# Hedgehog attention and an ELU feed-forward layer on one core: groups of four heads, DMA transposes and exact query maxima in place of head pairs and TensorE transposes

## Chip, cores and metric

The kernel runs on one core of a Trainium2 chip. The metric is the time of one execution on the device in microseconds (us); lower is better. TensorE is called PE below, VectorE DVE, ScalarE ACT, GpSimd POOL and SyncE SP.

## The reference

q, k and v are 8 batches x 8 heads x 576 tokens x 64, all float32.

```
def phi(x):                                   # x: b h s d
    proj = x @ w_phi                          # 64 -> 128
    proj = proj - max(|proj|, last axis)
    return concat([exp(proj), exp(-proj)])    # 256 features
q_p, k_p = phi(q), phi(k)
kv  = k_p^T v                                 # 256 x 64 for each head
z   = sum of k_p over the tokens
x   = (q_p kv) / (q_p z + 1e-6)               # tokens x 64
x   = heads side by side                      # 4608 x 512
h   = x @ moe_w_in                            # 512 -> 2048
g   = where(h > 0, h, exp(min(h, 0)) - 1)
out = g @ moe_w_out                           # 4608 x 512, float32
```

## The kernel before

**Attention** works on a pair of heads at a time (`emit_attention_pair`, 4 pairs x 8 batches = 32). Twelve DMAs on POOL's queue load q, k and v of the pair and cast them to bf16; token t*128+p goes to partition p, so that each run in DRAM is one token of one head, 64 floats or 256 bytes. PE transposes q and k against an identity (L198), ACT or DVE copies the result out (L199). For k, a matmul of K=128 against the zero-padded `w_phi_both` projects both heads of 128 tokens (L212); DVE takes the row maxima (L220), ACT the two exponentials (L227, L230) and exp(-m), exp(m) (L233, L237), and DVE multiplies v by them (L243). For q the projection comes out with features on partitions (L259) and ACT takes two exponentials (L266, L268); with `EXACT_QMAX = False` the maxima of q are not subtracted, so the two halves of q's features enter with equal weight. Then come kv (L276), the numerator and denominator (L341), the division on DVE (L351 to L353), a PE transpose of x (L369) and copies into `xT_sb` (L371, L375), which holds all 4608 tokens.

**Feed-forward** ("moe") works in 9 chunks of 512 tokens. `moe_mm1_unit` (16 in a chunk) does four matmuls of 512 columns (L102), exp on ACT (L110), min and subtract on DVE (L112) and a maximum with the PSUM tile on DVE (L116). `moe_mm2_unit` (4 in a chunk) does sixteen matmuls (L127), copies the result and stores it from SP's queue.

**Order.** Batches run in turn; after each pair some feed-forward units are emitted, `len(pending) // remaining_pairs` of them, so that few come early and many late. What is left follows at the end. The tile framework plans the final order on each engine at build time: it starts from this order and moves an instruction ahead where its inputs and buffers are ready in its plan. `nc.any` copies go to ACT or DVE as planned. PSUM has five banks for attention and three for feed-forward. Both weight matrices are loaded before the first pair (L84, L88), on the same queue as the pair's loads.

## Time and profile before

| | us |
|---|---|
| runs | 525.71, 530.53, 530.68 (median 530.53) |
| span of the profiled execution | 524.4 |
| PE busy | 408.5 (78%) |
| DVE busy | 364.1 (69%) |
| ACT busy | 319.5 (61%) |
| POOL busy | 258.3 (49%) |

The span runs from the first to the last instruction of one profiled execution. That execution's own time is not given beside it; the runs stand 1.3 to 6.3 us above the span, the median 6.1. The busy share of an engine is an average over stages that have different limits, so the rows below are taken stage by stage.

### The profile page before, as it was taken

Reading aid. Unit: us, or ns where it says so; the run is one execution under the profiler, and the core shown is the slowest. Engines: PE = TensorE matmul, PEld = TensorE weight load, DVE = VectorE, ACT = ScalarE, POOL = GpSimd, SP = SyncE. Lnnn points to the kernel's source line nnn. Section 1 sums busy time; section 2 is a strip of 40 time slices with the busy share of each in tenths; the row PEclk is TensorE's granted clock in tenths of the full one; section 3 lists DMA queues with packets and bytes.
Section 4 is the critical chain, followed back from the end, with each engine's and each line's share of the span. In section 5 each row is a group of like instructions: output and inputs, shape, how many; then the busy total and the mean of one; then the engine's idle time right before and its main releaser. Section 6 shows DMA issues by size and latency. Waiting matters only on the chain.

```text
span 524.4 us, 9742 instructions
## 1 busy us (share of the span) xinstructions
PE 408.5 (78%) x3200; PEld 222.5 (42%) x3200; DVE 364.1 (69%) x1358; ACT 319.5 (61%) x904; POOL 258.3 (49%) x400
## 2 busy tenths in 40 slices
PE   0056667678976679977789778977997999989997
PEld 0034444345543345534455444443544454434433
DVE  2055568989788988798986789479459579174470
ACT  0046568777568876787866788479257367153441
POOL 6299999967677767776676666460000000000000
PEclk9997668979989989998999899999999999989999
DMA  8989988955866756877567655660110100200102
GB/s 157 185 53 59 58 57 55 58 40 38 106 61 40 46 37 62 100 46 46 36 56 85 58 35 34 90 59 2 42 40 2 56 25 1 81 1 31 51 0 80
DMA packets 124817, 28.45 MB, mean 54 GB/s; under 512 B 117600, under 2 KB 119648, under 8 KB 124768
## 3 DMA queue, kind: packets, MB, share of 16 engines
q0 software_dynamic: 119584, 18.41, 47.7%
q1 hardware_dynamic: 5184, 9.44, 4.9%
q8 instruction: 25, 0.41, 0.3%
q14 instruction: 24, 0.20, 0.1%
HBM read 36.77 MB, written 9.44 MB: 88 GB/s over the span
## 4 chain that ended last, share of the span: by engine, by line
PE 49%; DVE 21%; ACT 21%; DMA 4%; issue 3%; POOL 1%; POOLq 0%; DVEq 0%; ACTq 0%
PE po L127 21%; PE ph L102 13%; DVE vs L243 5%; ACT EK L230 4%; ACT EK L227 4%; PE pk L212 4%; DVE gT L116 4%; DVE u_sb L112 4%; ACT Eq L266 4%; DVE x_pair L353 3%; DMA w_out_sb<-in_moe_w_out_dram 3%; PE pn L341 3%; PE tr L198 3%; ACT Eq L268 2%; PE xt L369 2%
## 5 line engine op out<-in xcount | busy, mean ns | idle before, releaser
L102 PE MATMUL ph<-xT_sb,w_in_sb 128*128 128x512 bf16 x576 | 158.9, 396 | 19.3 <-DVE gT L116 15.7
L127 PE MATMUL po<-w_out_sb,gT 128*128 128x512 bf16 x576 | 133.4, 379 | 0.3 <-DVE gT L116 0.2
L110 ACT ACTIVATE e_sb<-ph 128x512 f32<-128x512 f32 x144 | 85.2, 640 | 39.5 <-PE ph L102 39.1
L116 DVE TENSOR_TENSOR gT<-u_sb,ph 128x512 bf16<-128x512 bf16 x144 | 97.2, 681 | 1.8
L112 DVE TENSOR_SCALAR u_sb<-e_sb 128x512 bf16<-128x512 f32 x144 | 62.3, 442 | 42.4 <-ACT e_sb L110 41.8
L102 PEld LDWEIGHTS <-w_in_sb 128*128 128x128 bf16 x576 | 55.4, 101 | 75.8 <-issue 39.3
L243 DVE TENSOR_TENSOR vs<-v_aug,em 128x130 bf16<-128x130 bf16 (+1 forms) x384 | 75.6, 265 | 9.6 <-ACT em L233 9.1
L127 PEld LDWEIGHTS <-gT 128*128 128x128 bf16 x576 | 54.3, 98 | 59.6 <-issue 3.6
L168 POOL DMA_DIRECT2D q_pair<-in_q_dram x64 | 55.2, 866 | 43.4 <-PE tr L198 37.8
L266 ACT ACTIVATE Eq<-pq 128x288 bf16<-128x288 f32 x128 | 59.1, 462 | 24.6 <-PE pq L259 24.3
L220 DVE TENSOR_REDUCE m_k<-pk 128x4 f32<-128x512 f32 (+1 forms) x96 | 52.1, 594 | 14.3 <-PE pk L212 14.2
L268 ACT ACTIVATE Eq<-pq 128x288 bf16<-128x288 f32 x128 | 60.9, 476 | 0.0
L168 POOL DMA_DIRECT2D k_pair<-in_k_dram x64 | 57.1, 898 | 5.1 <-DMA w_out_sb<-in_moe_w_out_dram 4.4
L184 POOL DMA_DIRECT2D v_aug<-in_v_dram x64 | 53.7, 863 | 10.0 <-DVE den L351 5.2
L227 ACT ACTIVATE EK<-pk 128x512 bf16<-128x512 f32 (+1 forms) x96 | 52.5, 547 | 4.5 <-DVE m_k L220 4.5
L188 POOL DMA_DIRECT2D v_aug<-in_v_dram x64 | 40.8, 639 | 27.8 <-DVE vs L243 27.8
L276 PEld LDWEIGHTS <-EK 128*128 128x128 bf16 x640 | 32.4, 102 | 51.2 <-issue 20.1
L135 ACT COPY o_sb<-po 128x512 f32<-128x512 f32 x27 | 15.8, 586 | 62.0 <-PE po L127 62.0
L230 ACT ACTIVATE EK<-pk 128x512 bf16<-128x512 f32 (+1 forms) x96 | 53.5, 558 | 0.0
L259 PE MATMUL pq<-qTp,w_phi_both 128*128 128x288 bf16 x128 | 32.6, 300 | 19.9 <-ACT EK L230 18.6
L276 PE MATMUL pkv<-vs,EK 128*128 128x65 bf16 x640 | 36.1, 201 | 14.4 <-ACT EK L230 8.0
L174 POOL DMA_DIRECT2D k_pair<-in_k_dram x64 | 43.9, 685 | 4.5 <-DMA w_out_sb<-in_moe_w_out_dram 4.5
(46 smaller groups left out, 458.4 us busy)
## 6 DMA issues: line engine op xcount, KB each, us to landing
out_dram<-o_sb SPq DMA_DIRECT2D x36, 256.0 KB, 2.0
q_pair<-in_q_dram POOLq DMA_DIRECT2D x64, 64.0 KB, 2.6
k_pair<-in_k_dram POOLq DMA_DIRECT2D x64, 64.0 KB, 2.7
v_aug<-in_v_dram POOLq DMA_DIRECT2D x64, 64.0 KB, 2.8
w_in_sb<-in_moe_w_in_dram POOLq DMA_DIRECT2D x4, 512.0 KB, 7.1
w_out_sb<-in_moe_w_out_dram POOLq DMA_DIRECT2D x4, 512.0 KB, 15.9
q_pair<-in_q_dram POOLq DMA_DIRECT2D x64, 8.0 KB, 2.1
k_pair<-in_k_dram POOLq DMA_DIRECT2D x64, 8.0 KB, 2.3
```

The costliest lines, as they stand in the source:

```text
L102: nc.tensor.matmul(ph[:, 0:csz], w_in_sb[:, ct, jt * P:(jt + 1) * P], xT_sb[:, ct, t0:t0 + csz], start=(ct == 0), stop=(ct == N_CT - 1),)
L110: nc.scalar.activation(e_sb[:, 0:csz], ph[:, 0:csz], ACT.Exp)
L112: nc.vector.tensor_scalar(u_sb[:, 0:csz], e_sb[:, 0:csz], 1.0, 1.0, op0=ALU.min, op1=ALU.subtract,)
L116: nc.vector.tensor_tensor(gT[:, jt, 0:csz], u_sb[:, 0:csz], ph[:, 0:csz], op=ALU.max)
L127: nc.tensor.matmul(po[0:tsz], gT[:, jt, tt * P:tt * P + tsz], w_out_sb[:, jt, :], start=(jt == 0), stop=(jt == N_JT - 1),)
L168: nc.gpsimd.dma_start(out=dst[:, 0:full_st, hi * D:(hi + 1) * D], in_=src[b, h, 0:full_st * P, :].rearrange("(t p) d -> p t d", p=P),)
L227: nc.scalar.activation(EK[:, g0:g0 + gcnt, :, 0, :], pk_v, ACT.Exp, scale=1.0)
L230: nc.scalar.activation(EK[:, g0:g0 + gcnt, :, 1, :], pk_v, ACT.Exp, scale=-1.0)
L243: nc.vector.tensor_tensor(vs[hi][:, sg, g0:g0 + gcnt], v_aug[hi][:, g0:g0 + gcnt], em[:, sg, g0:g0 + gcnt, hi:hi + 1].to_broadcast((P, gcn ...
L266: nc.scalar.activation(eq[:, 0, c0:c0 + half_S], pq, ACT.Exp, scale=1.0)
L268: nc.scalar.activation(eq[:, 1, c0:c0 + half_S], pq, ACT.Exp, scale=-1.0)
L276: nc.tensor.matmul(pkv[:, hi, sg, :], EK[:, ti, hi, sg, :], vs[hi][:, sg, ti, :], start=(ti == 0), stop=(ti == n_st - 1),)
```

## The change

**Attention** works on groups of four heads (16 groups, two for each batch). One DMA per tensor and batch loads the first 512 tokens of all 8 heads, with token 4p+s on partition p, so that a run in DRAM is four tokens, 1 KB; two more load the last 64 tokens of each head. All transposes are DMA transposes on SP's queue: q and k (`transposes`), the query maxima (`mT`), and x straight into `xT_sb`; the identity, the PE transposes and their copies are gone. After a transpose, even and odd token blocks lie on partitions 0 to 63 and 64 to 127, and each projection is a matmul of K=64 on its half of the array's rows (`project`, `stage_q`). The maxima of q are computed (`stage_qmax`: a projection and a reduction as for k), split into a high and a low bf16 part, transposed, and subtracted in PSUM by matmuls with a matrix `sel` of -1 and 0. The multiplication of v moves from DVE to POOL. Exponentials and reductions act on 768 columns in two PSUM banks.

**Feed-forward.** The ELU becomes exp on ACT, min on POOL, and add and max in one DVE instruction. The sixteen matmuls of an output tile are cut into four parts. The copies of the output go to ACT. The store order follows the new token order.

**Order.** The pieces of group n are interleaved with those of group n+1, and 16 feed-forward units are spread over each group; a chunk joins the list four pieces after its batch. Loads run two batches ahead on POOL's queue. The first q and k are loaded before the weights. PSUM has two tiles of two banks for attention (`pj`) and four banks for feed-forward and kv.

```diff
+    def load_full(name, src, b, h0, h1):
+        if (name, b) not in natural:
+            natural[name, b] = (
+                io.tile([P, H, 4 * D], BF16, name=name + "f"),
+                io.tile([P, H // 2, D], BF16, name=name + "m"),
+            )
+        nc.gpsimd.dma_start(
+            out=natural[name, b][0][:, h0:h1, :],
+            in_=src[b, h0:h1, 0:FULL, :].rearrange("h (p s) d -> p h (s d)", s=4),
+        )
+    def load_mixed(name, src, b):
+        pairs = src[b, :, FULL:S, :].rearrange("(pr hi) p d -> hi p pr d", hi=2)
+        for hi in range(2):
+            nc.gpsimd.dma_start(
+                out=natural[name, b][1][hi * D:(hi + 1) * D, :, :], in_=pairs[hi]
+            )
...
+    for g in range(2):
+        for name, src in (("k", k), ("q", q)):
+            load_full(name, src, 0, g * GH, (g + 1) * GH)
+            if g == 0:
+                load_mixed(name, src, 0)
+    load("v", v, 0)
...
+    load("k", k, 1)
+    load("q", q, 1)
+    load("v", v, 1)
...
+    sel = consts.tile([P, NI, F], BF16)
+    nc.vector.memset(sel, 0.0)
+    for off in (0, NI, D, D + NI):
+        nc.gpsimd.affine_select(
+            out=sel, in_=sel, pattern=[[-1, NI], [0, F]],
+            compare_op=ALU.not_equal, fill=-1.0, base=-off, channel_multiplier=1,
+        )
...
+        e_sb = epool.tile([P, CHUNK], FP32, name="e_sb")
+        nc.scalar.activation(e_sb, ph, ACT.Exp)
+        nc.gpsimd.tensor_scalar(
+            e_sb, e_sb, 1.0, 0.0, op0=ALU.min, op1=ALU.max
+        )
+        nc.vector.scalar_tensor_tensor(
+            gT[:, jt, :], e_sb, -1.0, ph, op0=ALU.add, op1=ALU.max
+        )
...
+    def transposes(n):
+        if n >= NG:
+            return
+        b, g = divmod(n, 2)
+        for name in ("k", "q"):
+            full, mixed = natural[name, b]
+            dst = tpool.tile([P, NI, P], BF16, name=name + "T")
+            nc.sync.dma_start_transpose(
+                out=dst[:, 1:NI, :],
+                in_=full[:, g * GH:(g + 1) * GH, :].rearrange("p h x -> p (h x)"),
+            )
+            nc.sync.dma_start_transpose(
+                out=dst[:, 0:1, :],
+                in_=mixed[:, 2 * g:2 * g + 2, :].rearrange("p h x -> p (h x)"),
+            )
+            st[name + "T", n] = dst
+    def project(xT, c):
+        pj = pjp.tile([P, 2, 4, P], FP32, name="pj", tag="pj")
+        for i3 in range(3):
+            for par in range(2):
                 nc.tensor.matmul(
+                    pj[:, par, i3, :],
+                    xT[par * D:(par + 1) * D, 3 * c + i3, :],
+                    w2[par * D:(par + 1) * D, :],
                     start=True,
                     stop=True,
                 )
+        return pj[:, :, 0:3, :]
+    def stage_k(n, c):
...
+        pj = project(st["kT", n], c)
+        row_max(mk, pj, c)
+        for sg in range(2):
             nc.scalar.activation(
+                EK[:, sg, :, 3 * c:3 * c + 3, :], pj, ACT.Exp, scale=1.0 - 2.0 * sg
+            )
+        if c < 2:
+            return
...
+        nc.gpsimd.tensor_tensor(
+            vs[:, :, :, 0:D],
+            vf[:, g * GH:(g + 1) * GH, :]
+            .rearrange("p h (s d) -> p (h s) d", s=4)
+            .unsqueeze(1).to_broadcast((P, 2, 4 * GH, D)),
+            em[:, :, 2:2 * NI].unsqueeze(3).to_broadcast((P, 2, 4 * GH, D)),
+            op=ALU.mult,
+        )
+        nc.gpsimd.tensor_copy(vs[:, :, :, D], em[:, :, 2:2 * NI])
+        for hi in range(2):
+            r = slice(hi * D, (hi + 1) * D)
+            nc.gpsimd.tensor_tensor(
+                vsm[r, :, :, hi, 0:D],
+                vm[r, 2 * g:2 * g + 2, :].unsqueeze(1).to_broadcast((D, 2, 2, D)),
+                em[r, :, 0:2].unsqueeze(3).to_broadcast((D, 2, 2, D)),
+                op=ALU.mult,
+            )
+            nc.gpsimd.tensor_copy(vsm[r, :, :, hi, D], em[r, :, 0:2])
+    def stage_qmax(n, c):
...
+        pj = project(st["qT", n], c)
+        row_max(mq, pj, c)
+        if c < 2:
+            return
...
+        nc.sync.dma_start_transpose(out=mT, in_=mhl.rearrange("p r x -> p (r x)"))
+    def stage_q(n, c):
...
+        for par in range(2):
+            r = slice(par * D, (par + 1) * D)
+            nc.tensor.matmul(
+                pj[:, par, 0:3 * P],
+                w2[r, :],
+                qT[r, 3 * c:3 * c + 3, :].rearrange("p i t -> p (i t)"),
+                start=True,
+                stop=False,
+            )
+        for i3 in range(3):
+            for par in range(2):
+                r = slice(par * D, (par + 1) * D)
+                nc.tensor.matmul(
+                    pj[:, par, i3 * P:(i3 + 1) * P],
+                    sel[r, 3 * c + i3, :],
+                    mT[r, 0, :],
+                    start=False,
+                    stop=(i3 == 2),
+                )
+        for sg in range(2):
             nc.scalar.activation(
+                Eq[:, sg, :, 3 * c * P:3 * (c + 1) * P], pj[:, :, 0:3 * P], ACT.Exp,
+                scale=1.0 - 2.0 * sg,
+            )
+    def stage_pn(n, pr):
...
+        nc.sync.dma_start_transpose(
+            out=xT_sb[:, ct, full_col(b):full_col(b) + FULL].rearrange(
+                "p (t r) -> p t r", t=4
+            ),
+            in_=xp[:, 0:4].rearrange("p t h d -> p (t h d)"),
+        )
+        nc.sync.dma_start_transpose(
+            out=xT_sb[:, ct, mixed_col(b):mixed_col(b) + D].rearrange(
+                "p (t r) -> p t r", t=1
+            ),
+            in_=xp[0:D, 4].rearrange("p h d -> p (h d)"),
+        )
+    for n in range(NG):
...
+        pieces = []
+        for c in range(3):
+            pieces.append((stage_q, n, c))
+            if nxt:
+                pieces.append((stage_qmax, n + 1, c))
+        pieces.append((transposes, n + 2))
+        for pr in range(2):
+            pieces.append((stage_kv, n, pr))
+        if nxt:
+            pieces.append((stage_k, n + 1, 0))
+        pieces.append((stage_pn, n, 0))
+        if nxt:
+            pieces.append((stage_k, n + 1, 1))
+        pieces.append((stage_pn, n, 1))
+        if nxt:
+            pieces.append((stage_k, n + 1, 2))
...
+        for j, (fn, *args) in enumerate(pieces):
+            fn(*args)
+            after_piece()
+            want = 16 * (j + 1) // len(pieces)
+            while done < want:
+                emit_moe()
+                done += 1
```

## Rows read from the trace of the kernel before

**Rows 1.** The page's parts 1 and 2: busy us by engine; tenths in 40 slices.

```profile
PE 408.5 (78%) x3200; PEld 222.5 (42%) x3200; DVE 364.1 (69%) x1358; ACT 319.5 (61%) x904; POOL 258.3 (49%) x400
...
PE   0056667678976679977789778977997999989997
...
POOL 6299999967677767776676666460000000000000
...
DMA  8989988955866756877567655660110100200102
```

**Rows 2.** Timeline, first work of PE: start, us, engine, line, idle before.

```profile
26.93 0.69 PE L198 MATMUL tr<-ident,q_pair 128*128 128x128 bf16 x5 [26.93 <-DMA q_pair<-in_q_dram]
```

**Rows 3.** Busy us by stretch: PE, PEld, DVE, ACT, POOL; clock, DMA share, GB/s.

```profile
62.80:74.40 11.60, 7.17 (x70) 5.16 (x69) 7.01 (x33) 7.06 (x23) 11.60 (x19) 0.65 0.91 59
...
210.00:262.00 52.00, 40.94 (x384) 23.51 (x383) 45.15 (x181) 41.51 (x126) 36.77 (x56) 0.97 0.70 56
```

**Rows 4.** Chain of waits in the last feed-forward chunk: start, us, what.

```profile
504.46 1.02 PE ph L102 x4
```

**Rows 5.** Timeline of the end of the span: start, us, engine, line.

```profile
506.57 13.97 PE L127 MATMUL po<-w_out_sb,gT 128*128 128x512 bf16 x64
...
520.59 0.59 ACT L135 COPY o_sb<-po 128x512 f32<-128x512 f32 x1 [2.87 <-PE po L127]
```

**Rows 6.** Groups by line and shape, DVE, ACT, PE: count, busy us, mean ns.

```profile
L116 DVE TENSOR_TENSOR gT<-u_sb,ph 128x512 bf16<-128x512 bf16 x144 | 97.2, 681 | 1.8
L110 ACT ACTIVATE e_sb<-ph 128x512 f32<-128x512 f32 x144 | 85.2, 640 | 39.5 <-PE ph L102 39.1
L112 DVE TENSOR_SCALAR u_sb<-e_sb 128x512 bf16<-128x512 f32 x144 | 62.3, 442 | 42.4 <-ACT e_sb L110 41.8
...
L220 DVE TENSOR_REDUCE m_k<-pk 128x4 f32<-128x512 f32 x64 | 41.4, 684 | 14.3 <-PE pk L212 14.2
...
L227 ACT ACTIVATE EK<-pk 128x512 bf16<-128x512 f32 x64 | 39.1, 610 | 2.6 <-DVE m_k L220 2.6
L276 PE MATMUL pkv<-vs,EK 128*128 128x65 bf16 x640 | 36.1, 201 | 14.4 <-ACT EK L230 8.0 <-DVE vs L243 3.2 <-ACT Eq L266 1.6
...
L353 DVE TENSOR_TENSOR x_pair<-pn,rec 128x320 bf16<-128x320 f32 x64 | 31.3, 489 | 0.1
...
L227 ACT ACTIVATE EK<-pk 128x256 bf16<-128x256 f32 x32 | 13.5, 422 | 1.9 <-DVE m_k L220 1.9
L220 DVE TENSOR_REDUCE m_k<-pk 128x2 f32<-128x256 f32 x32 | 13.2, 413 | 0.0
...
L352 DVE RECIPROCAL rec<-den 128x5 f32<-128x5 f32 x64 | 11.8, 185 | 0.1
L284 DVE CAST kv_sb<-pkv 128x260 bf16<-128x260 f32 x26 | 11.0, 424 | 1.2 <-PE pkv L276 0.4
...
L351 DVE TENSOR_SCALAR den<-pn 128x5 f32<-128x5 f32 x64 | 9.8, 160 | 20.2 <-PE pn L341 20.1
```

**Rows 7.** Timeline, numerators of one pair on PE, middle of the span.

```profile
228.14 0.83 PE L341 MATMUL pn<-kv_sb,Eq 128*128 128x65 bf16 x20 [0.68 <-DVE kv_sb L284]
```

**Rows 8.** Groups by line and shape, POOL: loads of 512 and 64 runs, elementwise work.

```profile
L184 POOL DMA_DIRECT2D v_aug<-in_v_dram x64 | 53.7, 863 | 10.0 <-DVE den L351 5.2 <-DVE v_aug L183 1.7 <-DVE Eq L255 1.2
L188 POOL DMA_DIRECT2D v_aug<-in_v_dram x64 | 40.8, 639 | 27.8 <-DVE vs L243 27.8
...
masks.py:199 POOL TENSOR_SCALAR_AFFINE_SELECT ident<-ident 128x128 bf16<-128x128 bf16 x1 | 0.3, 310 | 0.1
masks.py:197 POOL MEMSET ident<- 128x128 bf16 x1 | 0.2, 205 | 0.3 <-POOLq L413 0.3
...
L413 POOL MEMSET const-float32-0.0<- 128x1 f32 x1 | 0.1, 94 | 0.3 <-issue 0.3
```

**Rows 9.** The page's part 3, DMA queues: packets, MB, share of 16 engines' span.

```profile
q0 software_dynamic: 119584, 18.41, 47.7%
q1 hardware_dynamic: 5184, 9.44, 4.9%
```

More of the change, by code (lines that the diff above doesn't have):

```diff
@@ new lines, in moe_mm2, with enqueue_chunk @@
+        if part == 3:
+            o_sb = opool.tile([P, DM], FP32, name="o_sb")
+            nc.scalar.copy(o_sb, po)
+            for r0, rn, rows in out_rows(ch * (CHUNK // P) + tt):
+                nc.sync.dma_start(out=rows, in_=o_sb[r0:r0 + rn])
+    pending = []
+    def enqueue_chunk(ch):
+        for jt in range(N_JT):
+            pending.append((moe_mm1, ch, jt))
+        for tt in range(CHUNK // P):
+            for part in range(4):
+                pending.append((moe_mm2, ch, tt, part))
@@ L252, in emit_attention_pair, with stage_kv @@
-        Eq = []
-        for hi in range(2):
-            eq = work.tile([P, 2, S_pad], BF16, name=f"Eq{hi}")
-            nc.vector.memset(eq[:, :, S:S_pad], 0.0)
-            for half in range(2):
-                c0 = half * half_S
-                pq = apsum.tile([P, half_S], FP32, name="pq", tag="ap")
+                Eq[:, sg, :, 3 * c * P:3 * (c + 1) * P], pj[:, :, 0:3 * P], ACT.Exp,
+                scale=1.0 - 2.0 * sg,
+            )
+    def stage_kv(n, pr):
+        EK, vs, vsm = st["EK", n], st["vs", n], vsm_bufs[n % 2]
+        kv = mpp.tile([P, 2, 2, D + 1], FP32, name="kv", tag="mp")
+        for hi in range(2):
+            hh = 2 * pr + hi
+            for sg in range(2):
+                for s in range(4):
+                    nc.tensor.matmul(
+                        kv[:, hi, sg, :],
+                        EK[:, sg, s % 2, 1 + 2 * hh + s // 2, :],
+                        vs[:, sg, 4 * hh + s, :],
+                        start=(s == 0),
+                        stop=False,
+                    )
@@ L360, in emit_attention_pair @@
-        if DEBUG_SINKS and b == 0 and pr == 0:
-            for nm, t in (("x_pair", x_pair), ("kv_sb", kv_sb), ("m_k", m_k),
-                          ("qTp", qTp), ("kTp", kTp),
-                          ("EK", EK), ("Eq0", Eq[0]), ("vs0", vs[0])):
-                if nm in DEBUG_SINKS:
-                    nc.gpsimd.dma_start(out=DEBUG_SINKS[nm], in_=t)
-        xt = apsum.tile([P, n_st, P], BF16, name="xt", tag="ap")
-        for ti in range(n_st):
-            nc.tensor.transpose(xt[:, ti, :], x_pair[:, ti, :], ident)
@@ new lines, with after_piece @@
+    transposes(0)
+    transposes(1)
+    for c in range(3):
+        stage_qmax(0, c)
+    for c in range(3):
+        stage_k(0, c)
+    LAG = 4
+    timers = []
+    def after_piece():
+        for t in list(timers):
+            t[0] -= 1
+            if t[0] <= 0:
+                enqueue_chunk(t[1])
+                timers.remove(t)
+    for n in range(NG):
+        b, g = divmod(n, 2)
+        nxt = n + 1 < NG
+        pieces = []
+        for c in range(3):
+            pieces.append((stage_q, n, c))
[12 more added lines that the diff above has]
+            pieces.append((stage_k, n + 1, 2))
+        if g == 0 and b + 2 < B:
+            load("k", k, b + 2)
+            load("q", q, b + 2)
+        if g == 1 and b + 2 < B:
+            load("v", v, b + 2)
+        done = 0
+        for j, (fn, *args) in enumerate(pieces):
+            fn(*args)
+            after_piece()
[3 more added lines that the diff above has]
+                done += 1
+        if g == 1:
+            last_col = full_col(b) + FULL - 1 if b % 2 else full_col(b) + FULL + D - 1
+            for ch in range(N_CHUNK):
+                tiles = range(ch * 4, ch * 4 + 4)
+                if max(2 * (t // 9) + (1 if t % 9 >= 4 else 0) for t in tiles) == b:
+                    timers.append([LAG if n + 1 < NG else 0, ch])
@@ L402 @@
+    after_piece()
+    while pending:
+        emit_moe()
 _INS = ['q', 'k', 'v', 'w_phi', 'moe_w_in', 'moe_w_out']
```

394 lines of the change are left out of this document (129 added, 265 removed).

## The prediction

> **What bounds the kernel now.** I read the shares and the 40 slices first, then the start, the early and middle stretches, and the end. No engine fills the span [rows 1], so there is one limit per stage. (1) PE does nothing for 26.9 us: its first transpose waits for a load queued behind both weight matrices [rows 2]. (2) Early, a pair of heads takes 11.6 us; POOL, which issues twelve loads per pair, is busy in all of it and the 16 DMA engines for 0.91, while DVE and ACT have 7 us of work [rows 3]. Runs of 256 bytes set this pace. (3) In the middle DVE is busy 45 of 52 us [rows 3]. (4) Late, the slices of PE are full and those of POOL empty [rows 1]; at the end the feed-forward layers stand alone. There one unit of the first layer takes 1.02 us on PE [rows 4], and DVE, whose two steps take 0.44 and 0.68 us [rows 6], holds it there; the 64 matmuls of a second layer take 13.97 us, 218 ns each or 0.87 us per unit of four [rows 5]. All 288 units of the kernel are 251 us if nothing holds PE.
>
> **The change, priced per group of four heads** (16 of them, replacing 32 pairs).
>
> PE. Numerators: 20 matmuls of 65 columns run in 0.83 us [rows 7], and one of that size takes 0.20 us from end to end [rows 6], so they start every (0.83 - 0.20)/19 = 33 ns; 80 of kv and numerators are 2.6 us. By columns (218 ns for 512), 128 columns are 55 ns and 384 are 164. The k and maximum projections are 36 x 55 = 2.0 us, the q projections 6 x 164 + 18 x 55 = 2.0 us. The PE transposes go. Attention is 6.6 us, sixteen feed-forward units 14.0: 20.6 us. I count nothing for two K=64 matmuls side by side; if all of them pair up, 2.0 us go.
> What a switch between K=64 and full-row work costs no row shows. A 65-column matmul takes 0.20 us but they start every 0.033, so an array that had to run empty would lose up to 0.17 us; nine K=64 pieces, 18 switches: 0 to 3 us per group. I take 1.5: PE needs 22 us.
> The Trainium skill ("TensorEngine Tiling (Array Packing)", Key Properties) says that changing the tiling mode drains TensorE. By that rule the full 3 us stand, 11 us more over the seven groups in which PE sets the pace; the gap between 0.20 and 0.033 us agrees that there is something to drain, and no row shows a drain itself.
>
> ACT. 512 columns take 610 ns and 256 take 422 [rows 6], so 768 take 798; twelve are 9.6 us. With two small exponentials (0.25 each by that line) and a first-layer exponential at 0.64, a group with 16 first-layer units has 20.3 us; with four output copies at 0.59 [rows 5] instead, 12.5.
>
> DVE. Reductions take 684 and 413 ns [rows 6], so 768 columns take 955; six are 5.7 us. Division of 640 columns is 489 + 320 x 1.06 = 828, with 160 + 185 + 424 for the small steps and the kv copy: twice 1.6. With 0.3 for the split of the maxima: 9.2 us. The combined ELU step reads the same columns as the old maximum, 0.68. First-layer group 20.1 us, other 9.2. What it loses is the multiplication of v, the memsets and one ELU step.
>
> POOL. Here the price is uncertain. Its rows are a memset of 128 columns (205 ns) and of one (94), and an affine select of 128 (310) [rows 8]: 0.87 or 1.69 ns per column. A min of 512 columns is then 0.54 us at the least and 0.96 by the arithmetic row, which I take as the nearest; that row is bf16, and if float32 cost double it would be 1.82. The v multiplication, 2048 columns at 1.69, is 3.6 us, with its small companions 5.0. Loads: 512 runs take 863 ns of POOL, 64 take 639 [rows 8], 0.5 ns per run; 1024 runs are 1.12 us and each of the two tails of 256 runs 0.74, so 2.6 us per tensor: k and q in one group, v in the next. A first-layer group has 16 x 0.96 + 5.0 + 5.2 = 25.6 us, the other 7.6.
> The Trainium skill ("GPSIMD Engine Reference", Performance versus the Vector engine) gives 4497 ns for a two-input operation of 2048 float32 elements. By it the v multiplication is 0.9 us dearer, some 15 us over the kernel; no row here has such an operation.
>
> DMA. Today's 119,584 load packets took 0.477 x 524.4 x 16 engines, 33.5 ns each, the 2 KB output packets 79 ns [rows 9]. Loads of a group fall from 6,912 runs to 1,536 of 1 KB (between the two, 55) and 768 short ones: 6.9 us of all 16 engines; outputs 1.6. Transposes add 28 blocks of 128x128, 3,584 rows of 256 bytes; no row shows one. As plain packets of that size they cost 7.5 us; at the output packets' rate per byte, 9.9 ns a row, 2.2. I take the dearer, since its rows have that size. Total 16 of some 24 us: hidden, at this price. On SP 9 transposes per group stand among the stores, in the order of their producers; q's and k's run a group ahead, and the maxima's transpose has seven pieces behind it as cover. If that cover fails, `stage_q` waits with PE, and ACT after it.
>
> **The sum.** Start: eight issues at about 0.7 us from 1.3 us on, and as long again for landing and transposing (an estimate): 12 us instead of 26.9. Six pieces of maxima and k for group 0: 12 us. Groups 0 and 1 have no feed-forward work; ACT needs 10 us and the two `pj` buffers, held 1.7 to 2.8 us by each of eleven pieces, 13: 14 each. (The granted clock was 0.65 in today's thin early stretch [rows 3]; PE's 6.6 us would be 10 at that clock, and still not the limit.) 52 us. Then 14 groups, alternately first-layer (POOL, 26) and second-layer (PE, 22): 336. Then two chunks alone: 32 units at 0.96 (POOL; PE would need 0.87) and 32 at 0.87: 58.6. From the last copy to the end of the span 524.4 - 520.6 = 3.8 [rows 5]. Sum 450 us against a span of 524.4. The median of the runs stands 6.1 above that span: **456 us**, 14% faster. The gain comes from an earlier start (15 us), from the end of the 256-byte runs' pace and DVE's, and from a shorter feed-forward tail; attention's PE work hardly shrinks (its transposes go, but the maxima of q are new work). Its own range is 430 to 490.
>
> **Rivals.**
> Faster, 0.18: POOL's min costs 0.54 and matmul pairs overlap. POOL then needs 18.8 us, ACT and PE about 20.5. 45 + 14 x 20.5 + 57 + 4 + 6 = 399; with 18.6 in second-layer groups 386. For: a min is one pass over its columns, as the memset is. Against: four engines within 10% of one another seldom overlap fully; today DVE reaches 45/52.
> Coupling, 0.17: four engines between 20 and 26 us per group, in a fixed order, fall to 85% (30 and 24, mean 27), and POOL's order at the start puts `sel` and the first v multiplication behind thirty loads, 13 us more. 65 + 378 + 59 + 10 = 512, range 490 to 524. Another 0.05 lies within 1% of today.
> Slower by POOL, 0.10: the min, which stands between ACT and DVE in every first-layer unit, costs p. The time is 6 + 309 + 144p (112p from seven groups, 32p from the tail), and passes 530 at p = 1.5 us. At 1.82 it is 577, and more if two inputs double the v multiplication too. For: 1.69 ns per column was seen at half the bytes. Against: the memset's 0.87.
> Slower by transposes, 0.07: a row of 256 bytes costs more than a plain packet. At 69 ns the DMA engines fill a group of 24 us; at 93 they need 29.3 us and the time reaches 530; at four times the packet price, 134 ns, it is 6 + 114 + 14 x 38.5 = 659.
> That K=64 pairs don't run together, that is, the change doesn't do what it says there, costs nothing against this sum, since none were counted.
>
> **Chances and range.** A difference of 1% is about what this measurement tells from none. Forecast 0.43, faster rival 0.18, coupling 0.17, same 0.05, slower 0.17: faster 0.78, same 0.05, slower 0.17. The range 395 to 540 leaves out a third of the faster rival (0.06) and most of the slower ones (0.13).
>
> **What would show it.** First matmul near 12 us; q's projections with ACT at about 0.80 per 768 columns and DVE at 0.96; a POOL row for `e_sb` near 0.96; a period of 48 us for two groups with PE busy above 0.85; DMA share near two thirds with transposes landing in a few us; a tail of two chunks near 58 us. I would be wrong if SP's waits head the list of waits, if POOL fills whole stretches, if PE waits for `pj` in most pieces, or if PE's K=64 work takes over 6 us of a group.

## The result: 493.65 us, and the profile after

The changed kernel takes 493.65 us (median of 4 runs, 493.03 to 493.98) against 529.11: ratio 0.935, 95% interval 0.930 to 0.940. That is 6.5% faster where 14% was forecast. Its profiled execution has a span of 492.0 us. Where some runs of a version below took over 1.5% longer than its fastest, its time is the median of the others. The page's parts 1 and 2 after, as in [rows 1]:

```profile
PE 374.0 (76%) x3337; PEld 189.2 (38%) x3392; DVE 238.0 (48%) x405; ACT 244.8 (50%) x405; POOL 236.3 (48%) x332
...
PE   0020345559699969996999699979988997999996
...
POOL 8224907163916490749165825633570357052340
...
DMA  8999996922985297429733964263231201110201
```

Subtract PE's busy time from the span: 524.4 - 408.5 = 115.9 us of idle PE before, 492.0 - 374.0 = 118.0 after. So nearly the whole gain is work that PE no longer does (34.5 us), and hardly any is idle time won. (Of the 3392 matmuls after, one for each weight load in the row, 55 left no record. Seven versions below with the same matmuls and all records show PE busy for 373.6 to 379.0 us, so 34.5 is too much by some 5 us at the most.) The slices show why: PE is emptier over the first eight than it was, and fuller behind them. The change bought a better steady state and paid part of it back at the start.

**The start.** Busy us by stretch, columns as in [rows 3] (to the third group; the regular groups; the tail):

```profile
0.00:99.50 99.50, 28.71 (x338) 18.75 (x341) 25.80 (x45) 24.62 (x36) 46.65 (x65) 0.97 1.19 142
99.50:432.00 332.50, 289.79 (x2747) 145.36 (x2795) 190.16 (x328) 195.81 (x329) 169.93 (x235) 0.94 0.48 79
432.00:492.00 60.00, 55.54 (x253) 25.04 (x256) 22.01 (x32) 24.42 (x41) 19.69 (x32) 1.00 0.13 45
```

The last two chunks stand alone from 432.0 us on. So the regular groups took 332.5 us where the sum had 336, the tail 60.0 where it had 62.4 with what follows the last copy. The start took 99.5 where the sum had 52, and PE was idle for 70.8 of it. A DMA share of 1.19, with 8 or 9 tenths in seven of the first eight slices, says that the DMA engines were busy nearly all that time. PE's long waits there (timeline, answering [rows 2]):

```profile
28.03 0.82 PE L232 MATMUL pj<-w,qT 64*128 64x128 bf16 x12 [28.03 <-DMA qT<-qm]
...
43.15 0.40 PE L232 MATMUL pj<-w,qT 64*128 64x128 bf16 x4 [6.04 <-DMA qT<-qf]
...
53.62 0.60 PE L348 MATMUL kv<-vs,EK 128*128 128x65 bf16 x8 [8.52 <-POOL vs L281]
...
94.39 1.86 PE L160 MATMUL ph<-xT_sb,w_in_sb 128*128 128x512 bf16 x4 [5.07 <-DMA xT_sb<-xp]
```

PE waits for transposes by DMA and for POOL. The DMA queues over the first 100 us (packets, MB, share of 16 engines), and how long transposes took there (count, median us from issue to landing):

```profile
q0 software_dynamic: 20304, 10.72, 86.6%
q1 hardware_dynamic: 13977, 3.35, 31.8%
...
kT<-kf SPq DMA_TRANSPOSE x5, 9.3
...
qT<-qf SPq DMA_TRANSPOSE x4, 11.8
...
mT<-mhl SPq DMA_TRANSPOSE x3, 7.9
```

Over the whole span the same transposes land in 3.2, 3.9 and 3.1 us (medians of 16). POOL's timeline shows its part:

```profile
8.80 1.34 POOL L85 DMA_DIRECT2D vm<-in_v_dram  x2
10.24 1.64 POOL L103 DMA_DIRECT2D w_in_sb<-in_moe_w_in_dram  x3
15.10 0.53 POOL L103 DMA_DIRECT2D w_in_sb<-in_moe_w_in_dram  x1 [3.22 <-DMA kf<-in_k_dram]
...
45.77 1.48 POOL L110 DMA_DIRECT2D w_out_sb<-in_moe_w_out_dram  x2 [2.13 <-DMA qf<-in_q_dram]
47.33 1.23 POOL L119 TENSOR_SCALAR_AFFINE_SELECT sel<-sel 128x1152 bf16<-128x1152 bf16 x1
48.52 3.63 POOL L273 TENSOR_TENSOR vs<-vf,em 128x2048 bf16<-128x2048 bf16 x1
```

The program gives POOL's loads eight semaphores in turn, and each issue waits for the landing of the eighth before it, so that never more than eight are on their way. The seventeenth is the first that loses time by it: ten such waits between 15 and 46 us, 25.4 us in all. In POOL's order the selector and the first multiplication of v stand behind them.

**The regular groups.** POOL, the forecast's bound for a first-layer group, is busy 27 of 48 us; PE is busy 42 (two windows of a pair of groups, columns as above):

```profile
205.00:229.00 24.00, 18.86 (x200) 9.51 (x202) 16.08 (x27) 15.36 (x26) 15.41 (x22) 1.00 0.51 67
229.00:253.00 24.00, 23.10 (x202) 11.39 (x206) 12.02 (x23) 13.39 (x22) 11.45 (x17) 0.93 0.84 130
```

One stall per chunk is left in them, at its end. On POOL:

```profile
219.55 0.99 POOL L77 DMA_DIRECT2D kf<-in_k_dram  x1 [1.41 <-PE pj L232]
220.56 3.65 POOL L273 TENSOR_TENSOR vs<-vf,em 128x2048 bf16<-128x2048 bf16 x1
...
228.11 1.77 POOL L169 TENSOR_SCALAR e_sb<-e_sb 128x512 f32<-128x512 f32 x3
```

and on PE, which waits 4.14 us and then runs seven matmuls in 2.62 us (1.53 at the 218 ns of [rows 5]; the granted clock is 1.00 from 229.5 to 230.1 us and 0.50 from there to 232, so the last four ran at the lower of the two levels, 1.2 GHz, behind the wait):

```profile
229.50 2.62 PE L182 MATMUL po<-w_out_sb,gT 128*128 128x512 bf16 x7 [4.14 <-DVE gT L172]
```

Three first-layer units stand in POOL's queue behind loads and the multiplication of v. Prices of the new shapes, columns as in [rows 6]:

```profile
L169 POOL TENSOR_SCALAR e_sb<-e_sb 128x512 f32<-128x512 f32 x144 | 87.9, 614 | 95.8 <-ACT e_sb L168 90.9
...
L273 POOL TENSOR_TENSOR vs<-vf,em 128x2048 bf16<-128x2048 bf16 x16 | 58.1, 3629 | 90.1 <-ACT em L266 82.8
L259 ACT ACTIVATE EK<-pj 128x768 bf16<-128x768 f32 x96 | 72.5, 811 | 49.7 <-DVE mk L242 49.4
...
L242 DVE TENSOR_REDUCE mq<-pj 128x6 f32<-128x768 f32 x48 | 45.8, 957 | 88.2 <-PE pj L232 88.2
```

One q piece between feed-forward matmuls, in this kernel and with K=128 matmuls in its place (run e4 below; timelines):

```profile
409.17 1.90 PE L160 MATMUL ph<-xT_sb,w_in_sb 128*128 128x512 bf16 x8
411.00 0.34 PE L318 MATMUL pq<-qT,w 64*128 64x384 bf16 x2
411.18 0.33 PE L328 MATMUL pq<-mT,sel 64*128 64x128 bf16 x6
411.44 1.04 PE L160 MATMUL ph<-xT_sb,w_in_sb 128*128 128x512 bf16 x4
```

```profile
407.48 1.03 PE L183 MATMUL po<-w_out_sb,gT 128*128 128x512 bf16 x4
408.35 0.49 PE L319 MATMUL pq<-qT,w 128*128 128x384 bf16 x2
408.67 0.50 PE L329 MATMUL pq<-mT,sel 128*128 128x128 bf16 x6
409.00 2.11 PE L183 MATMUL po<-w_out_sb,gT 128*128 128x512 bf16 x9
```

From start to start, two matmuls of 384 columns and six of 128 take 0.44 us in K=64 and 0.65 in K=128; by their columns they need 0.66 one behind the other and 0.33 in pairs. So pairs run side by side, and 0.11 us goes into the switch back. The switch in shows ahead of the piece: it starts 1.83 us after the first of eight 512-column matmuls, which need 1.74 at 218 ns, and in K=128 0.87 after the first of four, which need 0.87. So each of the two switches costs about 0.1 us where PE doesn't wait.

The DMA queues over the span, answering [rows 9]:

```profile
q0 software_dynamic: 40896, 18.39, 31.9%
q1 hardware_dynamic: 67200, 24.14, 25.9%
```

A load packet took 0.319 x 492 x 16 / 40,896 = 61 ns. Less the outputs' 411 us of [rows 9], the 62,016 packets of the transposes took 26 ns each.

### The profile page after: what moved, and what is told of

Its sections match the earlier page's. It is cut to its first block, busy times and chain, and to the rows that moved or that the text cites. A ratio compares the mean times of both kernels' runs of the same rounds, so it can differ in the third digit from the quotient of the medians.

```text
span 492.0 us, 8615 instructions
## 1 busy us (share of the span) xinstructions
PE 374.0 (76%) x3337; PEld 189.2 (38%) x3392; DVE 238.0 (48%) x405; ACT 244.8 (50%) x405; POOL 236.3 (48%) x332
## 3 DMA queue, kind: packets, MB, share of 16 engines
q0 software_dynamic: 40896, 18.39, 31.9%
## 4 chain that ended last, share of the span: by engine, by line
PE 40%; POOL 18%; DMA 12%; ACT 12%; issue 9%; DVE 8%; SPq 0%; POOLq 0%; ACTq 0%
PE po L182 18%; PE ph L160 11%; POOL vs L273 6%; ACT EK L259 5%; PE kv L348 4%; DMA qf<-in_q_dram 4%; ACT Eq L336 4%; DMA vm<-in_v_dram 3%; DVE gT L172 3%; POOL e_sb L169 3%; POOL vsm L284 2%; PE pj L232 2%; ACT e_sb L168 2%; PE pn L379 2%; DMA kT<-kf 2%
## 5 line engine op out<-in xcount | busy, mean ns | idle before, releaser
L182 PE MATMUL po<-w_out_sb,gT 128*128 128x512 bf16 x547 | 143.2, 398 | 24.5 <-DVE gT L172 22.4
L160 PE MATMUL ph<-xT_sb,w_in_sb 128*128 128x512 bf16 x550 | 139.7, 386 | 9.6 <-DMA xT_sb<-xp 5.4
L169 POOL TENSOR_SCALAR e_sb<-e_sb 128x512 f32<-128x512 f32 x144 | 87.9, 614 | 95.8 <-ACT e_sb L168 90.9
L172 DVE SCALAR_TENSOR_TENSOR gT<-e_sb,ph 128x512 bf16<-128x512 f32 x144 | 95.0, 684 | 76.8 <-POOL e_sb L169 76.5
L273 POOL TENSOR_TENSOR vs<-vf,em 128x2048 bf16<-128x2048 bf16 x16 | 58.1, 3629 | 90.1 <-ACT em L266 82.8
L259 ACT ACTIVATE EK<-pj 128x768 bf16<-128x768 f32 x96 | 72.5, 811 | 49.7 <-DVE mk L242 49.4
L336 ACT ACTIVATE Eq<-pq 128x768 bf16<-128x768 f32 x96 | 72.8, 835 | 40.6 <-PE pq L328 40.6
L242 DVE TENSOR_REDUCE mq<-pj 128x6 f32<-128x768 f32 x48 | 45.8, 957 | 88.2 <-PE pj L232 88.2
L160 PEld LDWEIGHTS <-w_in_sb 128*128 128x128 bf16 x576 | 50.6, 99 | 63.8 <-issue 11.6
L242 DVE TENSOR_REDUCE mk<-pj 128x6 f32<-128x768 f32 x48 | 45.7, 953 | 13.5 <-PE pj L232 13.0
L232 PE MATMUL pj<-w,qT 64*128 64x128 bf16 x288 | 18.6, 241 | 43.9 <-DMA qT<-qm 28.0
L348 PE MATMUL kv<-vs,EK 128*128 128x65 bf16 x512 | 29.9, 212 | 15.9 <-POOL vs L281 12.5
L379 PE MATMUL pn<-kv_sb,Eq 128*128 128x65 bf16 x640 | 26.8, 198 | 0.0
L391 DVE TENSOR_TENSOR xp<-pn,rec 128x640 bf16<-128x640 f32 x32 | 26.3, 823 | 0.9
```

The source lines that it names most:

```text
L160: nc.tensor.matmul(ph, w_in_sb[:, ct, jt * P:(jt + 1) * P], xT_sb[:, ct, t0:t0 + CHUNK], start=(ct == 0), stop=(ct == N_CT - 1),)
L169: nc.gpsimd.tensor_scalar(e_sb, e_sb, 1.0, 0.0, op0=ALU.min, op1=ALU.max)
L172: nc.vector.scalar_tensor_tensor(gT[:, jt, :], e_sb, -1.0, ph, op0=ALU.add, op1=ALU.max)
L182: nc.tensor.matmul(po, gT[:, jt, tt * P:(tt + 1) * P], w_out_sb[:, jt, :], start=(jt == 0), stop=(jt == N_JT - 1),)
L232: nc.tensor.matmul(pj[:, par, i3, :], xT[par * D:(par + 1) * D, 3 * c + i3, :], w2[par * D:(par + 1) * D, :], start=True, stop=True,)
L242: nc.vector.tensor_reduce(m[:, 3 * c:3 * c + 3, :].rearrange("p i r -> p r i"), pj, axis=AX.X, op=ALU.max, apply_absolute_value=True,)
```

## The experiments

All ratios are to the kernel before, on the same chip; its median was 526.7 to 529.5 us in the five rounds, so times of two rounds compare to about 0.5%. "Third group" is when the exponentials of its maxima begin (99.5 us in the changed kernel); it measures the start. In single executions it moves by itself: in run e5, whose edit begins with batch 2, the first matmul ran at 31.2 us instead of 28.0 and the third group at 98.1.

**Where did the start go?** First the weights' 4 MB of loads out (run e2):

```
-        nc.gpsimd.dma_start(out=w_in_sb[:, ct, :], in_=w_in_r[:, ct, :])
+    nc.vector.memset(w_in_sb, 0.0)          # w_out_sb likewise
```

> The two weight matrices of the feed-forward layer are filled with zeros on DVE instead of being loaded; the feed-forward output is then zero, all its instructions remain. Theory D: at the start the loads of two batches and both weight matrices fill the 16 DMA engines until about 75 us, so that each transpose lands after 8 to 12 us instead of 3, and POOL's queue stands still behind eight outstanding loads; weights are 4.2 MB of 10.7 MB moved in the first 100 us, so the first vs multiplication comes some 20 us earlier and the time falls by 20 to 30 us, to about 464 to 474. Rival O (order): POOL's order and the chain of handovers between groups 0 and 1 set the start; the time falls by less than 10 us.

472.50 us (median of two runs), 0.896 (0.888 to 0.903); third group at 80.2, regular groups unchanged. 19 us of the start are the weights' loads.

The selector's four steps moved ahead on POOL, behind the first load of v (run e3):

```
     load("v", v, 0)
+    sel = consts.tile(...); memset; four affine_selects
```

> The selector matrix is built on POOL right after the first v load is issued instead of after all thirty loads. In the changed kernel the first exponentials of q wait 20.9 us, of which the last 12 (45 to 57 us) for the selector. Theory O: the time falls by 8 to 14 us, to about 480 to 486. Theory D: the first v multiplication still comes at about 47 us, behind the last weight load, and with it kv and the numerators of group 0; the time falls by at most 5 us.

485.66 us, 0.920 (0.912 to 0.927); third group at 91.9. Worth 8 us: a part only. Group 0 takes 23.0 us instead of 38.3, group 1 31.3 instead of 24.6.

The loads of batch 1 and the weights made to wait for the first groups' maxima, by a one-column copy into their tiles (run e7):

```
+    gate(w_in_sb[:, :, 0:1], st["mk", 0][:, 5:9, 0:1])   # then the loads
+    load_gated("k", k, 1, st["mq", 0][:, 8, 0:1])        # q likewise; v, w_out: mk of group 1
```

> At the start the loads of batch 1 wait for the first maxima of q, the first weight matrix for the first maxima of k, and the v of batch 1 and the second weight matrix for the maxima of k of group 1, each by a one-column copy; the rest as in the changed kernel. Theory D: the first transposes meet only the loads of batch 0; PE's first matmul comes at 18 to 22 us instead of 28.0, the first group's v multiplication and selector no longer stand behind thirty loads, and the third group begins 15 to 25 us earlier; the time is 468 to 479. Rival O: the chain of handovers of groups 0 and 1 (transposes, maxima, their transposes, q, kv, numerators) sets it; the time falls by less than 10 us.

484.10 us, 0.915 (0.910 to 0.921); third group at 89.3, 10 us earlier where theory D had 15 to 25. Of these, 4 come until group 0's k is done, 6 in group 0 and none in group 1. That the held-back loads now meet these groups fits, but no run shows it apart.

All loads but batch 0's left out (its tiles are read again), weights zero (run e9):

```
     def load(name, src, b):
+        if b > 0:
+            natural[name, b] = natural[name, 0]
+            return
```

> Left out: the loads of batches 1 to 7 (their groups read the tiles of batch 0) and of both weight matrices (zeros). Theory D (the start was slow because the 10.7 MB of loads in the first 100 us fill the DMA engines and each transpose lands after 8 to 12 us): first matmul at 18 to 22 us, transposes land in about 3 us from the start, groups 0 and 1 take the 14 to 16 us of the sum, the third group begins by 62 (99.5 in the changed kernel), time 445 to 458. Rival C (a chain of handovers: maxima, split, transpose, q, kv, numerators, with no feed-forward work beside it): groups 0 and 1 still take 20 us or more each, third group at 70 to 80, time 465 to 475. In the steady groups the multiplication of v is still on POOL, so 22.5 and about 24.5 us stay in both.

461.06 us, 0.873 (0.870 to 0.877). The third group begins at 69.0, 30.5 us earlier; groups 0 and 1 take 18.3 and 18.6 us, between the two theories. First matmul and the issues of transposes on SP, in this kernel (timelines):

```profile
23.43 0.82 PE L231 MATMUL pj<-w,qT 64*128 64x128 bf16 x12 [23.43 <-DMA qT<-qm]
```

```profile
6.55 1.36 SPq L217 DMA_TRANSPOSE kT<-kf  x1
8.13 4.13 SPq L221 DMA_TRANSPOSE kT<-km  x2
12.30 1.41 SPq L217 DMA_TRANSPOSE qT<-qf  x1
13.80 2.52 SPq L221 DMA_TRANSPOSE qT<-qm  x2
```

So of the 47.5 us by which the start missed, 30.5 go with the loads of the weights and the later batches: their traffic, and on POOL their issues and waits, which no run takes apart. 17 are there without them: 8 until group 0's k is done, 4.5 in each of groups 0 and 1. In the first 8, batch 0's own loads still fill the DMA engines (share 1.18 in the first 20 us). The six transposes above landed 8.4 to 10.8 us after their issue, the last at 23.6; those issued after 20 us took 2 to 4. In its regular groups, without any load, 22.3 and 25.4 us stay: the multiplication of v alone keeps a stall of 3.15 us per chunk there.

The transposition of the split maxima left out (a constant tile of zeros is read; run e10):

```
-        nc.sync.dma_start_transpose(out=mT, in_=mhl.rearrange("p r x -> p (r x)"))
+        st["mT", n] = mT_const
```

> Left out: the transposition of the split maxima; the selector matmuls read a constant tile of zeros, everything else stays. If that hop is on the path of groups 0 and 1 (PE waited 5.0 us for it at 54 us where the loads were ordered), the third group begins 8 to 15 us earlier than 99.5 and the time is 479 to 486. If the loads and POOL's queue hold these groups anyway, the third group stays at 95 to 100 and the time at 490 to 494. Steady groups stay at 22.5 and 25.3 in both: there the hop has seven pieces of cover.

489.51 us, 0.927 (0.924 to 0.931); third group at 96.0. That hop is worth 3.5 us there at most: other late things hold these groups.

**What holds the regular groups?** The multiplication of v on DVE (run e1):

```
-        nc.gpsimd.tensor_tensor(vs[:, :, :, 0:D], ...
+        nc.vector.tensor_tensor(vs[:, :, :, 0:D], ...   # and its companions
```

> The multiplication of v by exp(-m), exp(m) moves from POOL to DVE; nothing else. Theory S (steady state): in the changed kernel the last three min operations of every first layer stand behind one v multiplication (3.6 us) and its companions on POOL, PE waits 4 us for them once per chunk and then runs some microseconds at the lower clock; without it the period of 24 us per group falls to about 21.5 and the time from 494 to about 455 to 465. DVE has 48% busy and takes about 2.7 us more per group. Rival L: the three load issues that stand on POOL in the same place are enough to hold PE; the wait shrinks to 2 to 3 us and the time stays above 480. Rival P: PE's own work (20.6 us and the switches) sets the period; the wait moves elsewhere and the time stays within 1% of 494.

484.07 us, 0.919 (0.913 to 0.924). The last five periods, which have no loads, are of 21.6 to 22.0 us; those with loads of 21.9 and 28 to 29. So rival L holds: the stall stays, with another cause (POOL's timeline in this kernel):

```profile
216.86 0.94 POOL L77 DMA_DIRECT2D kf<-in_k_dram  x1 [1.26 <-DMA kT<-kf]
224.22 1.23 POOL L85 DMA_DIRECT2D km<-in_k_dram  x2 [6.42 <-DMA kT<-km]
225.47 0.63 POOL L169 TENSOR_SCALAR e_sb<-e_sb 128x512 f32<-128x512 f32 x1
```

A load waits 6.42 us for its buffer, which a transpose still reads, and the min behind it waits too. Now the loads placed behind the mins instead, with v's multiplication back on POOL (run e5):

```
+            if fn is stage_kv and args[1] == 1 and g == 1 and b + 2 < B:
+                load_gated("k", k, b + 2, st["kv", n, 1][:, 0, 0, 0:1])   # q, v likewise
```

> From batch 2 on, the loads of k, q and v are held back by a one-column copy that depends on the second kv copy of the odd group, so that they stand on POOL after the min operations of a first layer and not among them; the v multiplication stays on POOL. In the run with the v multiplication on DVE, POOL stood 6.4 us at a load that waited for its buffer, with three min operations behind it. Theory V: in the changed kernel the v multiplication and its companions (5.2 us) alone hold the last three min operations; PE's wait of 4 us per chunk stays at 3 us or more, two groups still take 47 to 48 us, and the time is 484 to 494. Theory L: the load issues (2.9 us in the same place) are the larger part; two groups take 44 to 45 us and the time falls to 470 to 478.

497.98 us, 0.943 (0.937 to 0.948), above both theories. 3.15 us of stall per chunk stay, so the multiplication alone is enough for one, as the loads alone were in the run before. PE now also waits 16.8 us in nine waits for transposes of x (5.4 in two in the changed kernel), a cause that comes up again below. Both edits together (run e6):

```
+        nc.vector.tensor_tensor(vs[:, :, :, 0:D], ...        # run e1
+                load_gated("k", k, b + 2, ...)               # run e5
```

> Both: loads held back as in the run before it and the v multiplication on DVE. Theory queue: PE's stalls come from whatever stands before the last three min operations on POOL; with neither there, every group takes the 21.9 us that the groups without loads took when only the v multiplication was moved; from the third group on 14 x 2 us are gained against the changed kernel, and the time is 455 to 465. Rival P: another wait takes the place again and the time stays above 475.

474.39 us, 0.897 (0.891 to 0.904). POOL's stall is gone, but groups with loads still take 25 to 26.7 us, and the time is in neither forecast, just under the rival's 475. With the gated start as well (run e8):

```
+    gate(w_in_sb[:, :, 0:1], st["mk", 0][:, 5:9, 0:1])   # and the rest of run e7
```

> The held-back start, the held-back loads and the v multiplication on DVE together. If the two theories are right their gains add: 494 - 20 - 34, about 430 to 445, which would be below the predicted 456 because PE needs 21.9 us per group and not 24. Rival: the start and the steady state share a cause, and the sum of the gains is missed by more than 10 us.

467.62 us, 0.885 (0.881 to 0.889), third group at 82.2; the 25 to 26 us stay, and the sum of the gains is missed by over 20 us, as the rival had it. The list of PE's waits in this kernel (total us, times, longest) names the wait that took over, the transposes of x beside the bunched loads:

```profile
PE ph L176 <- DMA xT_sb<-xp: 20.0, 10, 7.7
```

**Is it the bunch?** The loads of k, q, v given out at three places of two groups (run e11):

```
+                if g == 0 and args[1] == 1:
+                    load_gated("k", k, b + 2, mark)
+                if g == 1 and args[1] == 0:
+                    load_gated("q", q, b + 2, mark)    # v: behind g == 1's last pn
```

> The 467.6 us version with the loads of k, q and v of a later batch given out at three places of a pair of groups instead of one. Theory B (nine load DMAs in a bunch delay the transposes of x, PE waits for xT 20 us in all): groups with loads fall from 25 to 26 us to 22.5 to 23.5, time 447 to 456. Rival (the sum of the traffic, not its bunching, delays the transposes, or a load in the middle of the first layer's mins brings POOL's stall back): periods add up to the same, time 464 to 475.

457.62 us, 0.867 (0.862 to 0.872): periods of 20.1 and 24 us. The bunch it was: PE's waits for x's transposes in the regular groups fell from 12.3 to 3.6 us (one long wait, 7.7 and 9.1 us, lies ahead of them in both). The gain is a little under the expected one since the start became slower (third group at 87.3). The other cure, a later release of the feed-forward work (run e12):

```
-    LAG = 4
+    LAG = 8
```

> The 467.6 us version with a chunk's feed-forward work released eight pieces after its last x instead of four. Theory B: the transposes of x have about 6 us more to land, PE's waits for xT (20 us in ten waits) fall below 8, and the later release costs 5 to 7 us once, at the end: 455 to 463. Rival (the transposes are late by more, or the wait goes to another transpose): periods of 25 to 26 stay and the late release is added: 468 to 475.

461.97 us, 0.873 (0.869 to 0.878): periods of 22.3 and 23.8, and PE's list of waits has none for x's transposes. Both cures together, and for batch 2 alone k's load moved back by a group (run e13):

```
+    LAG = 8                                            # run e12
+                if args[1] == 1 and (n == 1 or (g == 0 and b > 0)):   # run e11
+                    load_gated("k", k, b + 2, mark)
```

> Spread loads (from the second batch pair on) and the release after eight pieces together, on the 467.6 us version. If both cured the same wait for xT by different means, the start is that of the later release (fourth group at 97.9 us), the periods are those of the spread loads (20.1 and 24, mean 22.05), and the time is 462.0 - 12 x (23.05 - 22.05) = 450, range 446 to 454. Rival: the two gains are one and the same, periods of 22.3 and 23.8 stay and the time is 458 to 463.

467.99 us (median of three runs), 0.884 (0.879 to 0.889): slower than either, a clear miss of both readings. Then q's first loads and transposes ahead of k's (run e14):

```
-        for name in ("k", "q"):
+        for name in (("q", "k") if n == 0 else ("k", "q")):
```

> As the run before it, with the first loads and the first transposes of q ahead of those of k, since the maxima of q are computed first. If the first matmul (23 us where 12 was forecast) waits for the transposes as SP issues them one behind the other (1.4, 4.1, 1.4 and 2.5 us for the four of group 0, the last 7 us from issue to landing), it starts 4 to 7 us earlier, at 16 to 19, and the whole is 2 to 6 us faster than the run before it, less where k's projections then wait. If it waits for the landing of the loads alone, whatever their order, it stays at 22 to 23.5 and the time does not change.

463.85 us, 0.875 (0.872 to 0.879). In this kernel (timeline)

```profile
17.55 0.82 PE L248 MATMUL pj<-w,qT 64*128 64x128 bf16 x12 [17.55 <-DMA qT<-qm]
```

the first matmul starts 5.5 us earlier by order alone: it waits for q's transposes, which SP now issues at 6.5 us and not at 12.3, behind k's, as in the rows of run e9. The periods of 23.2 to 24 us here, against 20.1 and 24 to 25 in the next run, which takes back the late release alone, show that spread loads and the late release undo each other; PE then waits 9.8 us in all for ACT to free a `pj` buffer (`pj <- ACT Eq`), 2.4 in the run with the spread alone. Why is open. So the early release again (run e15):

```
-    LAG = 8
+    LAG = 4
```

> The run with q first, its feed-forward work released after four pieces again instead of eight. If spread loads with an early release give the periods of 20.1 and 24 (mean 22.1) and the start keeps its third group at 76 to 78, the time is 457.6 - (87.3 - 77) = 447, range 444 to 451. If the gain of the spread version's steady groups was paid for by its slow start (work that is left over from the start fills later groups), the time stays at 455 to 460.

**452.21 us**, 0.858 (0.853 to 0.863), the fastest version, 14.2% under the kernel before; third group at 81.0, then 20.1 and 24 to 25 us. The time lies between its two readings. Against the run with spread loads alone it has two edits: q first, and batch 2's k a group later. Last, the same with K=128 projections, weights and selectors padded with zeros (run e16):

```
-                    xT[par * D:(par + 1) * D, 3 * c + i3, :],
-                    w2[par * D:(par + 1) * D, :],
+                    xT[:, 3 * c + i3, :],
+                    w2[:, par, :],
```

> As the run before it, with the K=64 projections as K=128 ones, zero-padded weights and selectors. In the changed kernel this cost nothing in a steady group, where POOL held PE up. Here PE is busy over 0.9 of a steady group: by the pieces (0.33 against 0.27 us for k and the maxima, 0.66 against 0.44 for q) six and three of them make 1.0 us per group, 13 to 16 us in all, if PE is now the bound; 0 to 4 us if a handover between the engines still is.

453.66 us, 0.860 (0.856 to 0.865). The page's first part of the two kernels:

```profile
PE 362.0 (80%) x3337; PEld 184.9 (41%) x3392; DVE 305.4 (68%) x545; ACT 245.7 (55%) x405; POOL 160.1 (36%) x236
```

```profile
PE 377.9 (84%) x3337; PEld 218.6 (48%) x3392; DVE 304.4 (67%) x546; ACT 245.8 (54%) x405; POOL 159.7 (35%) x236
```

PE is busy for 15.9 us more, and the span is 1.5 us longer. A part of that is the start, which is 1.6 us shorter here: `w2` is now filled by a memset first, so the loads of `w_phi` wait for it and the first load of q goes ahead of them. From the third to the sixteenth group PE is busy for 11.6 us more and the time is 3.0 us longer. So most of the added work fell into time in which PE had waited: handovers between the engines, more than PE's work, still set the pace. The same edit made to the changed kernel alone (run e4):

> The K=64 matmuls of the projections and of the selector become K=128 matmuls with zero-padded weights and selector, the same number and columns (the output buffers go from three to two for room). Reading of the trace: two K=64 matmuls of 384 columns start 0.16 us before the next work instead of 0.33, so they run side by side, and a switch of shapes costs about 0.1 us. Theory side by side: PE loses about 2 us per group gained there and gets back about 1 to 2 us of switches; the time rises by 0 to 15 us, to 494 to 509. Rival drain: the switches cost the full 3 us per group that the prediction held possible; the time falls by 15 us or more.

488.17 us, 0.925 (0.919 to 0.930), which neither reading had. The regular groups take 22.5 and 25.3 us in both kernels; 3.4 of the 5 us gained came at the start, where the first load of k goes ahead of the loads of `w_phi` and the first matmul ran at 20.8. Row tiling bought little: between feed-forward matmuls a q piece with its switch in takes 0.54 us against 0.65, but a piece of k or of the maxima 0.37 (0.27 and the 0.1 ahead of it) against 0.34, so that nine pieces save under 0.2 us per group. It saves more only where PE waits anyway, since the switch in then falls into the wait.

## Why the prediction was wrong

Its sum against the spans: 450.4 + 47.5 (start) - 3.5 (groups) - 2.4 (tail) = 492.0, as measured. One term carries the miss. (The 6.1 us on top of it were wrong too, since they came from two different executions: the changed kernel's runs stand 1.9 to 2.0 us above their own spans.)

- **The failing step: the start, "52 us"**, made of "12 us instead of 26.9" and "14 each" for groups 0 and 1. The 12 us allowed 6 for landing and transposing together. In run e9, without the loads of the weights and the later batches, group 0's k and q landed 3.5 to 5.0 us after their issue, by 10.6 us; their six transposes, issued one behind the other until 16.3, took another 8.4 to 10.8 each to land: 23.4. With all loads it was 28.0. For the groups I counted ACT and the `pj` buffers only: without those loads they take 18.5 us, with them 38 and 24.6. The profile of before had the sign: a DMA share of 1.08 in the 27 us ahead of the first matmul. The change kept that traffic and put the first transposes into it.
- **DMA "hidden, at this price"** holds for the regular groups (share 0.48) and was never asked of the start, where the weights and two batches of q, k and v come at once. My bounds for a transpose's packet, 9.9 to 33.5 ns, held (26). What I priced was engine time; what counted was a hop's time to land.
- **The coupling rival** named the mechanism, selector and first multiplication of v "behind thirty loads", and priced it at 13 us. It took POOL's issues at their busy time; they also wait for earlier loads to land, 25.4 us. The measured time lies in its range, but its other half, groups of 27 us, did not come.
- **336 us for 14 groups** was nearly right (332.5) by luck. The min takes 0.61 us, not 0.96, so POOL is no bound (27 of 48 us), and the rival that the min makes the kernel slower falls. Attention needs (374.0 - 139.7 - 143.2) / 16 = 5.7 us of PE per group, not 8.1: pairs run together. The two savings were eaten by one stall of 3 to 4 us per chunk, from POOL's order, not its load (runs e1, e5 and e6).
- **The faster rival** had both its conditions met, a cheap min and overlapping pairs, and forecast 399. Even the fastest version has 22.1 us per group on average where that rival counted 18.6 to 20.5. Its "against" was the right one: four engines in a fixed order do not overlap fully.
- **The switch between K=64 and full-row work**: 1.5 us per group taken, out of 0 to 3. At about 0.1 us for each of 18 switches it is 1.8 where PE doesn't wait. The Trainium skill ("TensorEngine Tiling (Array Packing)", Key Properties) says that a change of tiling mode drains TensorE; the 0.1 us lost at each change agrees with a drain, at 0.6 of my price of 0.17.
- **"Attention's PE work hardly shrinks"** was wrong, and it is the gain. The feed-forward rows of PE before and after:

```profile
L102 PE MATMUL ph<-xT_sb,w_in_sb 128*128 128x512 bf16 x576 | 158.9, 396 | 19.3 <-DVE gT L116 15.7 <-DVE v_aug L182 1.4 <-ACT xT_sb L371 0.7
L127 PE MATMUL po<-w_out_sb,gT 128*128 128x512 bf16 x576 | 133.4, 379 | 0.3 <-DVE gT L116 0.2
```

```profile
L182 PE MATMUL po<-w_out_sb,gT 128*128 128x512 bf16 x547 | 143.2, 398 | 24.5 <-DVE gT L172 22.4
L160 PE MATMUL ph<-xT_sb,w_in_sb 128*128 128x512 bf16 x550 | 139.7, 386 | 9.6 <-DMA xT_sb<-xp 5.4
```

  What is left of PE's busy time for attention is 408.5 - 292.3 = 116.2 us before and 91.1 after: 25 us less, in a kernel whose PE idled as long as before. The other 9 of the 34.5 us lie in the feed-forward rows, whose 1152 matmuls are the same, but 55 records are missing after. In run e1, which has them all, these rows sum to 291.5, and 87.0 us are left for attention.
- **Prices** of ACT (811 and 835 against 798 ns), DVE (957 against 955) and v's multiplication (3.63 against 3.6 us) held. For the last, the Trainium skill ("GPSIMD Engine Reference", Performance versus the Vector engine) gives 4.5 us for float32; this one, in bf16, was faster.

What stays open: how the 30.5 us of the start divide between slow landing and POOL's waits, why spread loads and a late release undo each other, and which handovers make up the 4.5 us in each of groups 0 and 1 without those loads.

## What to carry to other kernels

Price a start by itself: a hop by DMA costs its time to land beside all that is loading then, and several hops in a row cost that several times, so ask for the first data in the order of first use and hold the rest back. In an in-order queue that mixes loads and arithmetic, look at what stands behind a load that must wait for its buffer; a lightly busy engine can still be the stall. And take PE's idle time before and after: it tells at once whether a gain is less work or less waiting, if the matmul records are as many as the weight loads. Before splitting the array's rows, count the switches: here they cost as much as most of the pieces gained.

## What the runs showed that was not expected

- POOL's load issues go over eight semaphores in turn, and each waits for the landing of the eighth before it (the sums stand with POOL's timeline above). So a long run of loads blocks the arithmetic behind it.
- A change between K=64 and full-row matmuls cost about 0.1 us each way; between feed-forward matmuls, zero-padded K=128 pieces of k and the maxima were no slower than the K=64 pairs (0.34 us against 0.37).
- The min of 512 float32 columns took 614 ns on average with v's multiplication on POOL and 674 in the fastest version, where that work is on DVE. The mean mixes two cases: the median there is 613, and the 17 of 144 over 700 ns, 0.79 to 1.53 us, all run while DVE works on v. The multiplication took 2.37 us on DVE and 3.63 on POOL.
- SP needs 1.1 to 1.6 us for the issue of most transposes; in the changed kernel it was held for 9.5 and 9.0 us at two of group 1's (17.2 to 35.8 us). The transpose of group 0's maxima, whose input was ready at 33.2 us, stood behind them until 35.9.
